# Attention and sticky mixture of experts on one core: the order of the tail's vector operations in the three early blocks, the place of two groups of small products, and the splitting of weight pieces

## The chip, the cores and the metric

The kernel runs on one core of a Trainium2 chip. The metric is the device time of one execution in microseconds. Three executions of the kernel before took 684.99, 685.71 and 685.96 us; the median, 685.71 us, is the time before. Apart from these one execution was profiled, and every view of the trace is of that one.

## The reference

Two stages follow one another. The first is attention for 8 batches and 8 heads of width 64. Each of 512 local tokens attends to 32 global tokens and to the local tokens at most 32 places away; each of the 32 global tokens attends to all 544. The outputs of all heads of a token stand side by side as a row of 512 numbers, 576 rows a batch, 4608 rows in all. The second stage sends each row through one of eight experts:

```python
logits = np.einsum('bsd,de->bse', x, w_gate)
local_gate = 1.0 / (1.0 + np.exp(-np.einsum('bsd,de->bse', x, w_local).squeeze(-1)))
out = np.zeros((B, S, D), dtype=np.float32)
for b in range(B):
    prev_e = -1
    for s in range(S):
        fresh_e = int(np.argmax(logits[b, s]))
        if s == 0 or local_gate[b, s] < 0.5:
            e = fresh_e
        else:
            e = prev_e if prev_e >= 0 else fresh_e
        prev_e = e
        ls = logits[b, s] - logits[b, s].max()
        p = np.exp(ls)
        p /= p.sum() + 1e-09
        h = np.maximum(x[b, s] @ w1[e], 0.0)
        out[b, s] = p[e] * (h @ w2[e])
```

An expert's w1 is 512 x 1024 and its w2 1024 x 512. Which expert a row takes depends on the rows before it, so the lists of rows per expert can only be complete when the last attention output is.

## The kernel before, in words

**Attention** fills roughly the first 229 us, unit by unit (a pair of heads of a batch). It is software-pipelined, and its last two units, the finishing of the last batch and the routing of its rows are not worked off there: they are collected in a generator, `Attn.tail`, that yields after each small chunk of work.

**Expert blocks.** A block takes 256 rows of one expert. Its first product, mm1 (L1274), runs over eight groups fc 0 to 7 of 128 columns of w1, of 12 matmuls each: four take the high half of the weights with the high half of x, four the low half of the weights, four the low half of x. All numbers are split in a high and a low part of reduced precision, so that three products together give the precision that is wanted. ACT makes the high part of the result (`hh`, L1276) and DVE the low part (`hl`, L1279). The second product, mm2 (L1287), runs over the same eight fc, three matmuls each, once for rows 0 to 127 (y0) and once for rows 128 to 255 (y1).

**Three early blocks** (i = 0, 1, 2) take rows of which the expert is known before the routing ends. Each has 24 places called hooks: hooks 0 to 7 behind the groups of mm1, 8 to 15 behind those of mm2 y0, 16 to 23 behind those of mm2 y1. I write (i, k) for hook k of block i. At a hook the kernel takes the next chunk of the tail, then `flush`es the subtraction that is pending, then splits new pieces as the table `SP[i][k]` says. The engines execute in the order in which this code issues, so the table and the yields of the tail fix each engine's order.

**Pieces.** A weight piece is a quarter of w1 or of w2 of an expert, 512 KB; a block needs eight. It is loaded to a `raw` buffer by a DMA on SP's queue, ACT casts its high half (L1173), and at the next hook's flush the low half is made by a subtraction (L1183), on DVE, or on POOL for two pieces split ahead of block 0. A flush frees the `raw` buffer and issues the next load. SP[2] names the pieces of the fourth block that are split within block 2.

**The tail**, in order: the last global unit's transposes (`g_t`) and its products with v (`g_av`, L342; its probabilities `ptg` come from ACT L332); the last local unit's transposes and products (`l_t`, L263; `l_av`, followed on DVE by L282, L284 and L287); the finishing of the outputs; the gate's keys (`keys`, L753, L824); ranking by a prefix scan (`pc`, L911) and products with ones (L875 to L884); probabilities (`probs`, L764 to L785); lists (`lists`, L924 and on); `kinds` (L1064 to L1087), eleven operations on DVE, the last of which writes `cnd`; and `rest`, the picking of the later lists: four groups of three DVE operations (L1000, L1002, L1004), each on 128 x 486 numbers, and then 34 small matmuls (L1010).

**The hint.** `cnd` holds for each of the eight blocks behind the early ones which case of a switch it takes. Every engine loads the first of them in a register at the same place of its program, ahead of mm2 y0 fc 4 of block 2:

```python
if mid and fc == 4:
    self.finish(True)
    while not self.known:
        self.take(next(self.tail))
    self.hint(i + 1)
```

Behind this, between the mm2 y1 groups of block 2, the rows of the fourth block are transposed four times (`xpose`, L1228, behind fc 2, 4, 5 and 6), each split by ACT (L1230) and DVE (L1231) into halves.

## Time and profile before

| what | value |
|---|---|
| median of three runs | 685.71 us (684.99 to 685.96) |
| the profiled execution's own time | 684.55 us |
| its span | 682.8 us |
| mean granted clock of TensorE | 0.995 |
| PE busy | 655.4 us, 96% of the span |
| DVE busy | 433.7 us, 64% |
| ACT busy | 342.1 us, 50% |
| POOL busy | 195.0 us, 29% |

A row of the timeline or of the list of groups gives start, duration, engine, line, operation, what it writes and reads, and how many instructions it stands for; a bracket at the end gives the idle time just ahead of it and what ended that. A row of the windows gives the stretch, its length, the busy time and instructions of PE, PE's weight loads, DVE, ACT and POOL, the granted clock, the DMA share and GB/s. A row of the waits gives the engine and line that waited, the one waited for, microseconds in total, how often, and the longest. Block 0 begins at about 229 us, block 1 at 267, block 2 at 290, and the fourth block at 323.

### The profile page before, as it was taken

To read this page: it belongs to the slowest core of one execution; us is meant where nothing else is said; L and a number is where in the kernel's file an instruction comes from. 1 tells how busy PE (TensorE), PEld (TensorE's weight loads), DVE (VectorE), ACT (ScalarE), POOL (GpSimd) and SP (SyncE) were. 2 spreads that over 40 slices of the span, in tenths; PEclk is the share of its full clock that TensorE was granted. 3 is DMA by queue.
4 is the path that set the end of the run, shared out by engine and by line. 5 is a ranking of instruction groups with operands and counts; after the bars stand their busy time and mean duration, and the time that the engine had idled before them with its cause. 6 is when DMAs were issued, how large, how long until landed. Compare 5 with 4: busy or idle time off the path is not lost.

```text
span 682.8 us, 18511 instructions
## 1 busy us (share of the span) xinstructions
PE 655.4 (96%) x7285; PEld 556.2 (81%) x7285; DVE 433.7 (64%) x1101; ACT 342.1 (50%) x614; POOL 195.0 (29%) x321
## 2 busy tenths in 40 slices
PE   8999999999999899998999899999999999999995
PEld 7778778777677787886987798989898989898994
DVE  7878778788887677988425553626374526355573
ACT  4555556555555574743427534435354425255563
POOL 7634334343324301031213304021123011133023
PEclk9999999999999999999999999999999999999998
DMA  8966967866757497766626674528283617265673
GB/s 321 405 217 249 336 216 305 316 247 237 303 188 291 135 353 255 259 206 200 254 89 223 212 246 151 183 82 265 86 297 120 235 63 236 93 218 182 222 276 102
DMA packets 42886, 151.47 MB, mean 222 GB/s; under 512 B 7837, under 2 KB 9117, under 8 KB 38560
## 3 DMA queue, kind: packets, MB, share of 16 engines
q1 hardware_dynamic: 35536, 126.92, 52.5%
q0 software_dynamic: 6832, 21.90, 9.5%
q8 instruction: 78, 1.28, 0.8%
q14 instruction: 152, 1.25, 0.6%
q10 hardware_dynamic: 288, 0.13, 0.1%
HBM read 130.55 MB, written 19.16 MB: 219 GB/s over the span
## 4 chain that ended last, share of the span: by engine, by line
PE 56%; DVE 6%; issue 1%; ACT 1%; POOL 0%; DVEq 0%; POOLq 0%; ACTq 0%
PE ps L1274 26%; PE ps L1287 23%; PE ps L1228 2%; PE ps L1293 2%; DVE wp L1183 1%; DVE wq L1183 1%; DVE xT L1002 0%; DVE xT L1000 0%; PE ps L1010 0%; DVE xl L1183 0%; ACT wp L1173 0%; DVE wp L1231 0%; POOL xa L1214 0%; DVE o L916 0%; DVE xl L1231 0%
## 5 line engine op out<-in xcount | busy, mean ns | idle before, releaser
L1306 POOL DMA_INDIRECT out_dram<-y,tk x39 | 40.8, 1045 | 309.5 <-ACT y L1305 221.7
L1287 PE MATMUL ps<-wp,wq 128*128 128x512 f32 x444 | 114.5, 403 | 1.0 <-ACT wq L1403 1.0
L1274 PE MATMUL ps<-wp,wp 128*128 128x256 f32 (+6 forms) x672 | 107.7, 320 | 0.0
L1274 PEld LDWEIGHTS ps<-wp,wp 128*128 128x128 f32 x672 | 103.5, 188 | 3.5
L1287 PEld LDWEIGHTS ps<-wp,wq 128*128 128x128 f32 x444 | 82.2, 190 | 18.1 <-ACT wq L1403 1.2
L1279 DVE SCALAR_TENSOR_TENSOR wq<-ps,wq 128x384 fp32r<-128x384 f32 (+4 forms) x112 | 43.5, 414 | 56.5 <-ACT wq L1276 48.0
L193 POOL TENSOR_SCALAR_AFFINE_SELECT qbd<-raw 64x512 f32<-64x512 f32 x62 | 44.3, 714 | 118.4 <-PE ps L246 92.2
L1276 ACT ACTIVATE wq<-ps 128x256 fp32r<-128x256 f32 (+6 forms) x80 | 36.9, 463 | 76.0 <-PE ps L1274 63.9
L246 PE MATMUL ps<-kx,qbd 128*64 128x128 f32 x1024 | 67.4, 275 | 1.3 <-issue 0.7
L1231 DVE TENSOR_TENSOR wp<-ps,wp 128x512 fp32r<-128x512 f32 x40 | 27.5, 691 | 58.3 <-ACT wp L1230 58.3
L257 ACT ACTIVATE pe<-pe 128x512 f32<-128x512 f32 x64 | 40.7, 636 | 43.8 <-DVE pe L253 43.8
L246 PEld LDWEIGHTS ps<-kx,qbd 128*64 128x64 f32 x1024 | 58.5, 138 | 2.1 <-POOL kx L193 1.1
L251 DVE TENSOR_REDUCE mx<-ps 128x4 f32<-128x512 f32 x64 | 43.8, 685 | 24.3 <-PE ps L246 24.1
L1183 DVE TENSOR_TENSOR wp<-raw,wp 128x1024 fp32r<-128x1024 f32 x47 | 57.0, 1217 | 2.9 <-ACT wp L1173 2.8
L1214 POOL DMA_INDIRECT xa<-xs,idx x42 | 50.2, 1194 | 18.8 <-issue 8.5
L1305 ACT ACTIVATE y<-ps,pp 128x512 f32<-128x512 f32 x35 | 24.2, 690 | 60.3 <-PE ps L1287 48.4
L1173 ACT CAST wp<-raw 128x1024 fp32r<-128x1024 f32 x49 | 50.9, 1047 | 1.3 <-ACT hh L1276 0.5
L1230 ACT CAST wp<-ps 128x512 fp32r<-128x512 f32 x40 | 23.5, 589 | 50.1 <-PE ps L1228 49.9
L253 DVE TENSOR_TENSOR pe<-ps,mx 128x512 f32<-128x512 f32 x64 | 44.0, 687 | 1.6
L279 PEld LDWEIGHTS ps<-v,pt 128*32 128x32 f32 x2048 | 33.1, 110 | 14.1 <-issue 7.9
L279 PE MATMUL ps<-v,pt 128*32 128x65 f32 x2048 | 41.7, 222 | 2.1 <-DVE xa L287 1.1
L193 POOL TENSOR_SCALAR_AFFINE_SELECT kx<-raw 128x384 f32<-128x384 f32 (+3 forms) x127 | 42.6, 368 | 3.1 <-DMA raw<-in_qk_dram 1.0
(296 smaller groups left out, 1188.2 us busy)
## 6 DMA issues: line engine op xcount, KB each, us to landing
raw<-in_w_dram SPq DMA_DIRECT2D x78, 512.0 KB, 4.4
v<-in_vw_dram SPq DMA_DIRECT2D x32, 1040.0 KB, 9.2
raw<-in_qk_dram SPq DMA_DIRECT2D x32, 528.0 KB, 7.8
xa<-in_w_dram SPq DMA_DIRECT2D x26, 512.0 KB, 4.2
xT<-in_w_dram SPq DMA_DIRECT2D x20, 512.0 KB, 5.1
xs<-xa SPq DMA_DIRECT2D x8, 1056.0 KB, 5.9
qgb<-in_qg_dram SPq DMA_DIRECT2D x8, 128.0 KB, 4.7
xa<-xs,idx POOLq DMA_INDIRECT x42
```

The costliest lines, as they stand in the source:

```text
L193: self.nc.gpsimd.affine_select(out=out, in_=in_, pattern=pat, compare_op=ALU.is_ge, fill=0.0, base=0, channel_multiplier=0)
L246: nc.tensor.matmul(sp[64 * t2:64 * t2 + 64, t], qbd[:, w], kf[:, f:f + P], start=False, stop=True, skip_group_check=True)
L251: nc.vector.tensor_reduce(out=mx, in_=st["sp"], axis=AX.X, op=ALU.max)
L253: nc.vector.tensor_tensor(out=st["pe"][:, 4 * hb:4 * hb + 4], in0=st["sp"], in1=mx.broadcast_to([P, 4, P]), op=ALU.subtract)
L279: nc.tensor.matmul(o[32 * w4:32 * w4 + 32, g, h], pt[:, 2 * g + w4 // 2, w4 % 2, h, :], v[:, w, h * (D + 1):(h + 1) * (D + 1)], start=True ...
L1173: nc.scalar.copy(out=hi, in_=raw)
L1183: (nc.gpsimd if pool else nc.vector).tensor_tensor(out=lo, in0=raw, in1=hi.bitcast(F32), op=ALU.subtract)
L1214: self.nc.gpsimd.indirect_dma_start(out=self.xr[j] if k == "early" else self.xr4[:, j], out_offset=None, in_=src, in_offset=bass.IndirectO ...
L1274: nc.tensor.matmul(ph, a[:, dc, fs], b_[:, dc, n0:n1], start=(n == 0), stop=(n == 11))
L1279: nc.vector.scalar_tensor_tensor(out=o[:, fc, c:c + b_ - a], in0=ph[:, a - n0:b_ - n0], scalar=0.0, in1=hh[:, fc, a:b_].bitcast(F32), op0= ...
L1287: nc.tensor.matmul(py, a[:, fc, js], b_[:, fs], start=(fc == 0 and k == 0), stop=(fc == 7 and k == 2))
L1306: sc = nc.gpsimd.indirect_dma_start(out=self.out, out_offset=bass.IndirectOffsetOnAxis(ap=tk[rows, js], axis=0), in_=y[rows], in_offset=No ...
```

## The change

Five edits touch only the order of the work; the operations are the same and equally many.

- In `tail`, `yield from lag(2)` stands for one yield ahead of `g_av`, and the yield behind `alloc_a` is gone. So the products with v move from hook (0,1) to hook (0,2), into the same chunk as `l_t`.
- In the ranking of the last batch, six yields are put between the scan and the ranking products. Three yields of this generator pass at one hook, so the products move two hooks, from (0,22) to (1,0), and what follows them in the tail (probabilities, lists, kinds) comes two hooks later too. Kinds move from hooks (2,5) to (2,8) to hooks (2,7) to (2,10).
- Three operations of `rest` come early: one behind each three operations of `kinds`. The other nine follow behind `kinds` as before, two a hook.
- `SP[0]`: the splits at hooks 1, 2, 3, 4 stand at 2, 3, 4, 5.
- `SP[2]`: hook 14 is dropped, so that six pieces of the fourth block are split within block 2, where it were seven.

```diff
--- before.py
+++ after.py
@@ -535,11 +535,10 @@
         b = B - 1
         fin = [x for x in fin if x[0] is not None]
         self.g_t(sg)
-        yield
+        yield from lag(2)
         self.g_av(sg)
         self.at2.close()
         moe.alloc_a()
-        yield
         self.l_t(sl, 0)
         self.l_t(sl, 1)
         yield
@@ -570,9 +569,12 @@
         self.f4(b, rt)
         yield from every(rt.lists(self.ps_o), 2)
         yield LISTS
-        yield from every(rt.kinds(), 3)
+        r = rt.rest(self.ps_o)
+        for _ in every(rt.kinds(), 3):
+            next(r)
+            yield
         yield KINDS
-        yield from every(rt.rest(self.ps_o), RE)
+        yield from every(r, RE)
@@ -871,6 +873,7 @@
             nc.vector.tensor_copy(self.sumA, pc[:, :, n - 1])
             yield
         else:
+            yield from lag(6)
             cp = po()
@@ -1530,9 +1533,9 @@
-SP = [_sp({1: 1, 2: 1, 3: 1, 4: 1, 6: 1, 7: 1, 10: 1, 13: 1, 15: 1, 19: 1}),
+SP = [_sp({2: 1, 3: 1, 4: 1, 5: 1, 6: 1, 7: 1, 10: 1, 13: 1, 15: 1, 19: 1}),
       _sp({0: 1, 1: 1, 2: 1, 3: 1, 5: 1, 7: 1, 8: 1, 11: 1, 13: 1, 15: 1, 17: 1, 19: 1}),
-      _sp({1: 1, 3: 1, 5: 1, 7: 1, 10: 1, 12: 1, 14: 1})]
+      _sp({1: 1, 3: 1, 5: 1, 7: 1, 10: 1, 12: 1})]
```

In the changed file the lines behind the first edits have numbers three higher or so: L1274 is L1277 there, L1183 is L1186, L1279 is L1282, L1287 is L1290.

**Three places in the engines' order.** The first is DVE in block 0, behind mm1 fc 1. L345 to L349 finish the products with v, L1279 is the low part of a group of mm1, L1183 the subtraction of a piece, and L282 to L287 finish the last local unit. Before:

```order
L345 TENSOR_SCALAR rsg_125<-ps_69 128x1
L347 RECIPROCAL rsg_125<-rsg_125 128x1
L349 TENSOR_SCALAR xg_111<-ps_69,rsg_125 128x64
L1279 SCALAR_TENSOR_TENSOR hl<-ps_63,hh 128x256
L1183 TENSOR_TENSOR wp_4271<-raw_79,wp_4271 128x1024
L1279 SCALAR_TENSOR_TENSOR hl<-ps_65,hh 128x256
L282 TENSOR_SCALAR rs_123<-ps_70 128x4
L284 RECIPROCAL rs_123<-rs_123 128x4
L287 TENSOR_TENSOR xa_109<-ps_70,rs_123 128x2x128
L1183 TENSOR_TENSOR wp_4272<-raw_80,wp_4272 128x1024
```

And with the change:

```order
L1282 SCALAR_TENSOR_TENSOR hl<-ps_63,hh 128x256
L345 TENSOR_SCALAR rsg_125<-ps_69 128x1
L347 RECIPROCAL rsg_125<-rsg_125 128x1
L349 TENSOR_SCALAR xg_111<-ps_69,rsg_125 128x64
L1282 SCALAR_TENSOR_TENSOR hl<-ps_65,hh 128x256
L282 TENSOR_SCALAR rs_123<-ps_70 128x4
L284 RECIPROCAL rs_123<-rs_123 128x4
L287 TENSOR_TENSOR xa_109<-ps_70,rs_123 128x2x128
L1186 TENSOR_TENSOR wp_4285<-raw_79,wp_4285 128x1024
L1282 SCALAR_TENSOR_TENSOR hl<-ps_66,hh 128x256
```

The three operations behind the products with v now stand behind the low part of fc 2, and the third piece (index 2) is subtracted where the fourth was, behind the finishing of the local unit.

The second is PE between the last groups of block 0 and the first of block 1, with the ranking products. Before:

```order
L1287 MATMUL ps_64<-wp_4377,hh 128x512 x2
L1287 MATMUL ps_64<-wp_4377,hl 128x512
L875 LDWEIGHTS on
L875 MATMUL ps_69<-sumA,on 128x8
L876 LDWEIGHTS on
L876 MATMUL ps_69<-pc,on 128x8
L881 LDWEIGHTS nlt
L881 MATMUL ps_70<-oh,nlt 128x104
```

And with the change:

```order
L1290 MATMUL ps_64<-wp_4374,hh 128x512 x2
L1290 MATMUL ps_64<-wp_4374,hl 128x512
L1277 MATMUL ps_65<-xh,wq_4375 128x256 x8
L1277 MATMUL ps_65<-xl,wq_4375 128x256 x4
L878 LDWEIGHTS on
L878 MATMUL ps_69<-sumA,on 128x8
L879 LDWEIGHTS on
L879 MATMUL ps_69<-pc,on 128x8
L884 LDWEIGHTS nlt
```

The products now stand behind mm2 fc 7 of block 0 and behind the whole of mm1 fc 0 of block 1.

The third is DVE in block 2, around the operations of `kinds`. The L1279 with ps_66 that stands in both pieces is the one of fc 7, the last of mm1. Before:

```order
L1183 TENSOR_TENSOR wp_4271<-raw_78,wp_4271 128x1024
L1279 SCALAR_TENSOR_TENSOR hl<-ps_66,hh 128x256
L1078 TENSOR_SCALAR kb<-kq 1x8
L1081 TENSOR_SCALAR kt<-kq 1x8
L1083 TENSOR_TENSOR kt<-kt,kb 1x8
L1085 SCALAR_TENSOR_TENSOR kt<-left,kt 1x8
L1087 TENSOR_TENSOR cnd<-kt,kb 1x8
L1183 TENSOR_TENSOR wp_4272<-raw_79,wp_4272 128x1024
L1000 TENSOR_TENSOR xT<-cid,phi 128x9x54
```

And with the change, from the same L1279 on, first up to the subtraction:

```order
L1282 SCALAR_TENSOR_TENSOR hl<-ps_66,hh 128x256
L1067 TENSOR_SCALAR eid<-ek 1x13
L1069 TENSOR_TENSOR eoh<-ge 128x104
L1071 TENSOR_SCALAR cnd<-lim 1x1
L1003 TENSOR_TENSOR xT<-cid,phi 128x9x54
L1074 TENSOR_SCALAR kq<-cn 1x8
L1076 TENSOR_SCALAR kq<-kq 1x8
L1078 TENSOR_SCALAR kq<-kq 1x8
L1005 TENSOR_TENSOR xT<-xT,t_266 128x9x54
L1186 TENSOR_TENSOR wp_4286<-raw_79,wp_4286 128x1024
L1081 TENSOR_SCALAR kb<-kq 1x8
```

and then to the end of `kinds`:

```order
L1084 TENSOR_SCALAR kt<-kq 1x8
L1086 TENSOR_TENSOR kt<-kt,kb 1x8
L1007 TENSOR_SCALAR xT<-xT,ipf 128x9x54
L1088 SCALAR_TENSOR_TENSOR kt<-left,kt 1x8
L1090 TENSOR_TENSOR cnd<-kt,kb 1x8
L1003 TENSOR_TENSOR xT<-cid,phi 128x9x54
L1005 TENSOR_TENSOR xT<-xT,t_266 128x9x54
```

All eleven operations of `kinds`, three of `rest` and a subtraction now stand between the low part of fc 7 and the `cnd` that the hint loads; before it were the last five of `kinds`.

## The prediction

> **What bounds the kernel now.** I first read the page's busy times: PE is the engine that sets the end.
>
> ```profile
> PE 655.4 (96%) x7285; PEld 556.2 (81%) x7285; DVE 433.7 (64%) x1101; ACT 342.1 (50%) x614; POOL 195.0 (29%) x321
> ```
>
> The change leaves the work of PE as it is, and so it can only move PE's idle time and what hangs on it. Next I cut the span into windows by block, and listed the waits of PE from 226 to 323 us, the stretch that the change touches.
>
> ```profile
> 290.00:323.00 33.00, 28.42 (x234) 25.03 (x233) 27.80 (x59) 14.18 (x22) 8.60 (x7) 1.00 0.66 205
> PE ps L1228 <- DVE wp L1231: 2.2, 1, 2.2
> PE ps L1274 <- DVE hl L1279: 1.7, 1, 1.7
> PE ps L342 <- ACT ptg L332: 1.7, 1, 1.7
> PE ps L876 <- DVE pc L911: 1.1, 1, 1.1
> ```
>
> Block 2 (290 to 323) has DVE busy for 27.80 of 33.00 us: there DVE is nearly as full as PE (28.42). Two of the four large waits are on DVE's backlog there. Four waits sum to 6.7 us, about 1% of the span; the edits are put at three of them (L342, L876, L1228). A wait that is removed pays only if nothing stands right behind it. So I walk each place in order of time, with the lateness of PE against before carried along.
>
> **The products with v, one chunk later.**
>
> ```profile
> 235.27 0.93 PE L342 MATMUL ps<-v,ptg 128*32 128x65 f32 x48 [1.66 <-ACT ptg L332]
> 237.08 0.74 PE L1274 MATMUL ps<-xh,wp 128*128 128x256 f32 x4 [0.20 <-POOL wp L1183]
> 234.65 2.37 POOL L1183 TENSOR_TENSOR wp<-raw,wp 128x1024 fp32r<-128x1024 f32 x1 [4.37 <-DVE gx L785]
> ```
>
> The wait of 1.66 us looks like the prize. But the group of mm1 that comes behind (fc 2) needs the low half of its piece, which POOL finishes at 234.65 + 2.37 = 237.02, and PE does start it at 237.08, after a last wait of 0.20. Before, the products filled part of the time until then. Moved behind fc 2 they leave that time idle, since fc 2's low weights come no earlier. So nothing is gained, and the products' own time (235.27 to the next group's start 0.87 later) is added behind: **+0.9**. Its bounds are 0 (if POOL were to start earlier; its 4.37 of idle end with an operation of DVE that doesn't move) and +0.9.
>
> **Pieces split one hook later in block 0.** The products with v and the finishing of the local unit stand ahead of the subtraction of the third piece in DVE's new order, and its place is where the fourth piece's is now.
>
> ```profile
> 241.11 1.22 PE L1274 MATMUL ps<-xh,wp 128*128 128x256 f32 x8
> 239.09 1.22 DVE L1183 TENSOR_TENSOR wp<-raw,wp 128x1024 fp32r<-128x1024 f32 x1
> 241.84 0.42 DVE L287 TENSOR_TENSOR xa<-ps,rs 128x256 f32<-128x256 f32 x1
> 242.19 1.22 DVE L1183 TENSOR_TENSOR wp<-raw,wp 128x1024 fp32r<-128x1024 f32 x1
> 267.10 11.53 PE ps L1274 x96
> ```
>
> PE begins fc 4, the first group of the third piece, at 241.11, or 241.98 with the 0.87 before. A matmul takes 11.53 / 96 = 0.12, so the four with the high half last until 242.5. The low half came at 239.09 + 1.22 = 240.3, well ahead. Now it starts behind L287, at 242.19 + 0.87, and ends 1.22 later, at 244.28. PE waits 244.28 - 242.46 = **+1.8**. The bounds are +0.9 (L282 to L287 don't depend on the later products, so the 0.87 may not be added in full) and +1.8; I take the upper one, because L279, which they read, is behind the products on PE. DVE and PE then run equally late, so the fourth piece adds no further wait. The flush also issues the next load on SP's queue, one hook, some 1.5 us, later:
>
> ```profile
> raw<-in_w_dram SPq DMA_DIRECT2D x78, 512.0 KB, 4.4
> ```
>
> A load lands in 4.4 us and is not needed before block 0's mm2, over 5 us later; I cost it at nothing, and at up to 1.5 if that cover is gone. Together PE is now 2.7 us late.
>
> **The ranking products, two hooks later.**
>
> ```profile
> 264.72 0.18 PE L875 MATMUL ps<-sumA,on 128*128 128x8 bf16 x1
> 265.58 0.38 DVE L911 TENSOR_TENSOR_SCAN pc<-segb,rv 128x104 bf16<-128x104 f32 x1
> 266.01 0.17 PE L876 MATMUL ps<-pc,on 128*128 128x8 bf16 x1 [1.10 <-DVE pc L911]
> ```
>
> The scan ends at 265.96, at worst 2.7 later: 268.7. The products now stand behind mm2 fc 7 (three matmuls at 0.23, from the nine in 2.11 shown below: 0.7) and a whole group of twelve (1.44): 264.72 + 2.7 + 0.7 + 1.44 = 269.6. The wait goes: **-1.1**, and nothing takes its place here. PE is 1.6 late.
>
> **What follows the ranking moves into DVE's full stretch.**
>
> ```profile
> 265.87 0.18 DVE L764 TENSOR_TENSOR lpr<-L,lm 128x40 f32<-128x40 f32 x1
> 268.99 0.43 DVE L1279 SCALAR_TENSOR_TENSOR hl<-ps,hh 128x256 fp32r<-128x256 f32 x1 [1.79 <-ACT hh L1276]
> 270.43 0.42 DVE L1279 SCALAR_TENSOR_TENSOR hl<-ps,hh 128x256 fp32r<-128x256 f32 x1 [0.61 <-ACT hh L1276]
> 296.21 1.08 DVE L1279 SCALAR_TENSOR_TENSOR hl<-ps,hh 128x256 fp32r<-128x256 f32 x3
> ```
>
> DVE's operations for the probabilities ran from 265.87 to 268.99 - 1.79 = 267.20, ahead of an idle time of 1.79. Two hooks later these 1.3 us stand behind the low part of mm1 fc 0, and only the 0.61 ahead of fc 1 is still free; behind 270.43 DVE goes without a break to the three low parts at 296.21 for which mm1 of block 2 waits 1.7. DVE gets there 1.6 (PE's lateness) + 1.3 later, less what the 0.61 absorbs: 2.3 to 2.9; I take 2.6, **+1.0** on PE beside the 1.6. The bounds are 0 (all absorbed) and +1.3.
>
> **`kinds`, three operations of `rest` and the hint.** From the order: behind the low part of fc 7 DVE now has all of `kinds`, three operations of `rest` and a subtraction before `cnd` is written.
>
> ```profile
> 303.10 0.15 DVE L1064 TENSOR_SCALAR eid<-ek 1x13 int32<-1x13 f32 x1
> 303.35 0.14 DVE L1068 TENSOR_SCALAR cnd<-lim 1x1 int32<-1x1 f32 x1
> 304.45 0.15 DVE L1071 TENSOR_SCALAR kq<-cn 1x8 int32<-1x8 int32 x1
> 305.02 1.21 DVE L1183 TENSOR_TENSOR wp<-raw,wp 128x1024 fp32r<-128x1024 f32 x1
> 306.15 0.41 DVE L1279 SCALAR_TENSOR_TENSOR hl<-ps,hh 128x256 fp32r<-128x256 f32 x1
> 306.49 0.15 DVE L1078 TENSOR_SCALAR kb<-kq 1x8 f32<-1x8 int32 x1
> 307.12 0.16 DVE L1087 TENSOR_TENSOR cnd<-kt,kb 1x8 int32<-1x8 f32 x1
> 308.35 0.66 DVE L1000 TENSOR_TENSOR xT<-cid,phi 128x486 bf16<-128x486 bf16 x1
> 309.04 0.67 DVE L1002 TENSOR_TENSOR xT<-xT,t 128x486 bf16<-128x486 bf16 x1
> 309.74 0.36 DVE L1004 TENSOR_SCALAR xT<-xT,ipf 128x486 bf16<-128x486 bf16 x1
> 308.52 0.72 PE L1287 MATMUL ps<-wq,hh 128*128 128x512 f32 x2 [0.68 <-ACT wp L1173]
> ```
>
> The wait of 0.68 at 308.52 is named after ACT, but ACT's cast is not what comes last: it is the place of the hint, `cnd` was written at 307.28, and PE goes on 1.24 later. So this wait hangs on `cnd`. Its new time: the low part of fc 7 begins at 306.15 + 2.6 = 308.75. Behind it come by these rows 0.34, 0.39, 0.57 and 0.79 for itself and the three parts of `kinds`, 0.66 + 0.67 + 0.36 of `rest` and 1.13 to 1.21 of the subtraction: 4.9 to 5.0. Neighbours on DVE overlap (1.21 us of a subtraction take 1.13 from start to start), so I take 4.5, with 4.2 and 5.0 as bounds. `cnd` is written at 313.25, PE goes on at 314.5 instead of 308.52: 6.0 late, of which **+3.4** is new here. PE would arrive at 307.84 + 2.6 = 310.4 and idle for 4.0 us instead of 0.68. Behind the same load stand ACT and POOL, whose program holds it too; ACT's casts and `hh` are finished ahead of it, so nothing else becomes late by more than PE.
>
> **The fourth block's transposes, and six pieces.**
>
> ```profile
> 316.88 1.22 DVE L1183 TENSOR_TENSOR xl<-raw,xh 128x1024 fp32r<-128x1024 f32 x1
> 318.01 1.28 DVE L1231 TENSOR_TENSOR wp<-ps,wp 128x512 fp32r<-128x512 f32 x2
> 318.75 0.66 PE L1228 MATMUL ps<-idf,xa 128*128 128x128 f32 x4 [2.23 <-DVE wp L1231]
> ```
>
> The third transpose waits for the first L1231, which stands behind DVE's backlog. With PE 6.0 late the transpose comes at 318.75 - 2.23 + 6.0 = 322.5. DVE has, behind `cnd`, nine operations of `rest` (three times 1.7) and a subtraction (1.1), with small ones some 7 us: free at 320.3, and the first L1231 done by 321. This wait goes: **-2.2**. That a seventh subtraction (1.22 at 316.88) is gone from this stretch helps nothing any more; with that piece the slack of 1.5 would still do. The seventh piece is now split in the fourth block, whose mm2 needs it tens of microseconds later, and each later block again splits eight, so I cost it at nothing (1.1 if DVE were late there).
>
> Sum: 0.9 + 1.8 - 1.1 + 1.0 + 3.4 - 2.2 = **+3.8** us.
>
> **The clock.** Idle time of 4.0 us has a price of its own here, seen later in the same trace:
>
> ```profile
> 374.00:378.00 4.00, 1.65 (x10) 0.93 (x10) 3.66 (x6) 2.99 (x7) 0.00 (x0) 1.00 0.91 294
> 378.00:382.00 4.00, 3.50 (x9) 2.76 (x10) 1.53 (x2) 0.00 (x0) 0.00 (x0) 0.60 0.83 302
> 378.50 3.90 PE ps L1287 x9
> 402.56 2.11 PE ps L1287 x9
> ```
>
> After a stretch in which PE was busy for 1.65 of 4.00 us (41%) the granted clock fell to 0.60 on the mean of the next 4 us, and nine matmuls took 3.90 us where the chain has 2.11 for the same nine elsewhere: a loss of 1.8. An idle time of 4.0 leaves some stretch of that length with PE idle for at least half of it wherever the stretches begin, so I expect one such drop behind the hint: **+1.8** (bounds 0 and 1.8). The Trainium skill, "TensorE: Matmul & The Clock Gate", section "What's actually happening", says that the clock halves after at least one idle window of about 3.4 us, and that these windows run freely. Read strictly, a window with a matmul in it would not count; the drop in this trace, after a stretch with 41% of work, speaks for a looser reading. By the strict one an idle time of 4.0 us holds a whole window in about one case of five only, and the sum would stay at +3.8; that is the first rival.
>
> **Forecast**: +3.8 + 1.8 = +5.6 on the profiled execution's 684.55 us (span 682.8), about 690.1; the profiled execution lay 1.2 below the median, so on 685.71 it is **691.2** (rounded down, as most of the bounds lie lower). The work behind block 2 keeps PE as full as before, so no later slack returns it.
>
> **Rivals.**
> - *No drop of the clock.* For it: the two recorded halves of one idle time may fall into two stretches that each have enough work. Against: the row above. 685.7 + 3.8 = 689.5.
> - *Two or three drops.* The waits in block 0 (POOL's piece, 2.5 us idle around 236, and 1.8 at 243) and at mm1 of block 2 (1.7 + 1.0 = 2.7) are idle times of over 40% of such a stretch too. Each costs 1.2 to 1.8 more: 692.5 to 694.
> - *DVE's idle time takes in what is moved.* If the third piece is subtracted in time and `cnd` comes no later, because DVE reaches `kinds` early (it had 0.63 to 1.79 of idle ahead of some low parts), only the products' 0.9 is left: 686.6, no change that can be told.
> - *The named waits simply go*, the other side: L342, L876 and L1228 lose 1.66 + 1.10 + 2.23 with no lateness put in their place, so that PE is ahead and the hint's load is met in time: 680.7. It decides if `cnd` is written before PE arrives, that is, if the eleven operations of `kinds` begin before fc 7's low part. Against: the order puts all eleven behind it, and 4.5 us on DVE stand against 2.8 us that PE needs for the twelve matmuls of mm2 fc 0 to 3.
> - *A load comes late.* The issue of the next weights moves a hook, 1.5 us, in block 0: +1 to +2 on the forecast, 692 to 693.
>
> **How the numbers follow.** Forecast 0.42, no drop 0.20, more drops 0.20, late load 0.04, no change 0.08, faster 0.06. A difference of less than 0.2% (1.4 us, that is 684.3 to 687.1) can't be told from no change. The likeliest case's own range is 690.0 to 692.3: the bounds of the hint's 4.2 to 5.0, of DVE's backlog and of the third piece. The range of eight in ten reaches down past the case with no drop and its bounds and up to the second drop: 687.8 to 693.9. Chances: faster 0.06, same 0.08, slower 0.86.
>
> **What would show it.** In the profile of the changed kernel: at fc 4 of block 0 PE waits some 1.8 us for DVE's subtraction, and the wait of L342 is gone while fc 2 still ends its wait on POOL; no wait at the ranking products; at mm1 of block 2 a wait on the low part of 2.5 or so; behind fc 3 of mm2 in block 2 about 4 us of idle PE, whatever releaser is named, with `cnd` written some 1.2 ahead of its end; then a stretch of half clock; and L1228 without a wait. I am wrong on the price if `cnd` comes before 311, and on the clock if the windows behind the hint show 1.00.

## The result

The changed kernel takes 690.03 us (median of ten executions, 687.47 to 695.13), the kernel before 685.45 us beside it (683.36 to 688.42). The ratio is 1.0071 with a 95% interval of 1.0052 to 1.0089: slower by 4.6 us, within 3.6 to 6.1. Put beside the kernel before a second time, it gave 1.0067 (1.0046 to 1.0088). The forecast was 691.2 us, 5.5 above.

The profiled execution took 688.34 us, its span 686.6. The waits of PE from 226 to 328 us in the changed kernel, to be laid beside the four of before:

```profile
PE ps L1290 <- DVE xT L1003: 3.3, 1, 3.3
PE ps L1277 <- DVE hl L1282: 2.4, 1, 2.4
PE ps L1277 <- POOL wp L1186: 2.1, 2, 1.7
PE ps L1277 <- DVE wp L1186: 1.7, 1, 1.7
PE ps L1277 <- ACT wp L1176: 1.0, 1, 1.0
```

Three of the waits of before are gone from the list (the products with v, the ranking products, the fourth block's transposes). In their place stand two at mm1 fc 2 of block 0, one for ACT's cast (1.0) and one for POOL (1.7 of the 2.1), so that PE still waits where it waited ahead of the products with v; one at mm1 fc 4 of block 0 (1.7); and one at the hint (3.3 where it was 0.7). The one at mm1 of block 2 grew from 1.7 to 2.4. The rows in PE's order of time:

```profile
233.70 0.74 PE L1277 MATMUL ps<-xh,wp 128*128 128x256 f32 x4 [1.00 <-ACT wp L1176]
236.13 1.23 PE L1277 MATMUL ps<-xh,wp 128*128 128x256 f32 x4 [1.69 <-POOL wp L1186]
238.14 1.39 PE L342 MATMUL ps<-v,ptg 128*32 128x65 f32 x48
244.89 0.74 PE L1277 MATMUL ps<-xh,wp 128*128 128x256 f32 x4 [1.66 <-DVE wp L1186]
271.69 0.18 PE L879 MATMUL ps<-pc,on 128*128 128x8 bf16 x1
301.54 1.22 PE L1277 MATMUL ps<-xh,wp 128*128 128x256 f32 x8 [2.45 <-DVE hl L1282]
316.03 0.72 PE L1290 MATMUL ps<-wq,hh 128*128 128x512 f32 x2 [3.34 <-DVE xT L1003]
323.88 0.60 PE L1231 MATMUL ps<-idf,xa 128*128 128x128 f32 x4
```

L342, L879 and L1231 have no bracket any more. On DVE, these are the low part of fc 7 and the last operation of `kinds`, which writes `cnd`:

```profile
310.43 0.42 DVE L1282 SCALAR_TENSOR_TENSOR hl<-ps,hh 128x256 fp32r<-128x256 f32 x1
314.64 0.15 DVE L1090 TENSOR_TENSOR cnd<-kt,kb 1x8 int32<-1x8 f32 x1
```

From the one's start to the other's end are 4.36 us (forecast 4.5, before 1.13), and PE goes on at 316.03, 1.24 after `cnd`, as before. The low part of fc 6, just ahead, waits for ACT in both kernels, here before and with the change:

```profile
304.11 0.42 DVE L1279 SCALAR_TENSOR_TENSOR hl<-ps,hh 128x256 fp32r<-128x256 f32 x1 [0.63 <-ACT hh L1276]
```

```profile
308.96 0.42 DVE L1282 SCALAR_TENSOR_TENSOR hl<-ps,hh 128x256 fp32r<-128x256 f32 x1 [1.60 <-ACT hh L1279]
```

**The clock.** In windows of 4 us the changed kernel shows half clock at two places of block 0, and none behind the hint:

```profile
233.00:237.00 4.00, 1.60 (x8) 1.40 (x9) 1.46 (x7) 1.97 (x5) 2.35 (x1) 0.85 0.01 2
237.00:241.00 4.00, 4.00 (x68) 3.68 (x68) 1.03 (x4) 1.18 (x3) 0.00 (x0) 0.72 0.98 305
245.00:249.00 4.00, 4.00 (x49) 3.70 (x50) 2.15 (x5) 1.32 (x2) 0.00 (x0) 0.63 0.55 200
314.00:318.00 4.00, 1.97 (x9) 1.65 (x10) 3.88 (x11) 1.05 (x1) 0.00 (x0) 1.00 0.71 232
```

In windows of 1 us every such stretch of every profile adds up to 3.4 us at half clock, or to twice that. The profile before has one ahead of the program's end (at 378), the changed kernel three (235, 246, and 382 in the half case).

**Where the time went.** The waits and the places between them can be laid side by side by a few rows that every profile has: the start of POOL's second subtraction (L1183), the keys' transposes (L824), the first group of block 1, the group of mm1 in block 2 that waits for DVE, the row at which PE goes on behind the hint, the fourth block's first group, and the first group of the block behind the half case. Differences of their starts, in us; a star is a stretch of half clock that falls into it:

| from, to | before | before again | after | after again |
|---|---|---|---|---|
| POOL's subtraction, keys (block 0) | 24.48 | 26.13* | 30.21** | 28.83* |
| keys, block 1 | 7.81 | 7.79 | 6.28 | 6.27 |
| block 1, the group that waits in block 2 | 29.74 | 29.73 | 31.32 | 31.31 |
| that group, PE behind the hint | 11.84 | 11.83 | 14.49 | 14.50 |
| hint, fourth block | 14.16 | 14.17 | 11.73 | 13.35* |
| fourth block, behind the half case | 64.25* | 64.27* | 63.45* | 63.72* |

Where no star differs, repeated profiles agree within 0.02 us in all but the last row. So the waits belong to the order of the work; the stretches of half clock come and go. Without them block 0 takes 27.4 (the run with `rest` behind `kinds`, below, which is the changed kernel in all that stands ahead), and the change comes to +2.9 - 1.5 + 1.6 + 2.65 - 2.4 - 0.8 = **+2.4 us**. Between the two first profiles this leaves 1.4 us: two stretches of half clock in block 0 add 2.8 (30.21 against 27.4), 0.9 is saved ahead of POOL's subtraction, in the attention, which no edit touches, and 0.5 behind the last matmul. Together that is 3.8, the difference of the spans (686.6 and 682.8). Between the medians, 4.6 apart, the other 2.2 can only be put down to the clock by its mean; "Adding up" below does that.

### The profile page after: what moved, and what is told of

Its sections match the earlier page's. It is cut to its first block, busy times and chain, and to the rows that moved or that the text cites. A ratio compares the mean times of both kernels' runs of the same rounds, so it can differ in the third digit from the quotient of the medians.

```text
span 686.6 us, 18494 instructions
## 1 busy us (share of the span) xinstructions
PE 658.7 (96%) x7285; PEld 559.6 (81%) x7285; DVE 432.6 (63%) x1100; ACT 340.8 (50%) x613; POOL 195.8 (29%) x321
## 4 chain that ended last, share of the span: by engine, by line
PE 56%; DVE 6%; issue 1%; DMA 1%; SPq 1%; ACT 1%; POOL 0%; POOLq 0%
PE ps L1290 25%; PE ps L1277 25%; PE ps L1231 3%; PE ps L1296 2%; DVE wp L1186 2%; DVE wq L1186 1%; DMA xs<-gx 1%; DVE hl L1282 1%; SPq L420 1%; PE ps L1415 0%; PE ps L1013 0%; POOL xa L1217 0%; DVE o L919 0%; DVE xl L1234 0%; ACT wp L1176 0%
## 5 line engine op out<-in xcount | busy, mean ns | idle before, releaser
L1290 PE MATMUL ps<-wp,wq 128*128 128x512 f32 x444 | 114.4, 403 | 1.0 <-ACT wq L1406 1.0
L1277 PE MATMUL ps<-wp,wp 128*128 128x256 f32 (+6 forms) x672 | 107.7, 320 | 0.0
L1277 PEld LDWEIGHTS ps<-wp,wp 128*128 128x128 f32 x672 | 103.5, 188 | 3.5
L1290 PEld LDWEIGHTS ps<-wp,wq 128*128 128x128 f32 x444 | 82.3, 191 | 18.2 <-ACT wq L1406 1.2
L1282 DVE SCALAR_TENSOR_TENSOR wq<-ps,wq 128x384 fp32r<-128x384 f32 (+4 forms) x112 | 43.3, 412 | 58.5 <-ACT wq L1279 54.3
L1279 ACT ACTIVATE wq<-ps 128x256 fp32r<-128x256 f32 (+6 forms) x80 | 37.0, 464 | 75.9 <-PE ps L1277 64.5
L1186 DVE TENSOR_TENSOR wp<-raw,wp 128x1024 fp32r<-128x1024 f32 x38 | 46.1, 1216 | 2.8 <-ACT wp L1176 2.8
L1176 ACT CAST wp<-raw 128x1024 fp32r<-128x1024 f32 x40 | 41.4, 1045 | 3.6 <-DVE xT L1003 3.6
```

The costliest lines, as they stand in the source:

```text
L1176: nc.scalar.copy(out=hi, in_=raw)
L1186: (nc.gpsimd if pool else nc.vector).tensor_tensor(out=lo, in0=raw, in1=hi.bitcast(F32), op=ALU.subtract)
L1277: nc.tensor.matmul(ph, a[:, dc, fs], b_[:, dc, n0:n1], start=(n == 0), stop=(n == 11))
L1282: nc.vector.scalar_tensor_tensor(out=o[:, fc, c:c + b_ - a], in0=ph[:, a - n0:b_ - n0], scalar=0.0, in1=hh[:, fc, a:b_].bitcast(F32), op0= ...
L1290: nc.tensor.matmul(py, a[:, fc, js], b_[:, fs], start=(fc == 0 and k == 0), stop=(fc == 7 and k == 2))
```

## The experiments

Each of the first four undoes one part of the changed kernel.

**Block 0 undone, both edits:**

```diff
-        yield from lag(2)
+        yield
         self.g_av(sg)
         self.at2.close()
         moe.alloc_a()
+        yield
-SP = [_sp({2: 1, 3: 1, 4: 1, 5: 1, 6: 1, 7: 1, ...
+SP = [_sp({1: 1, 2: 1, 3: 1, 4: 1, 6: 1, 7: 1, ...
```

> The changed kernel with both edits of block 0 undone (products with v one chunk earlier, splits at hooks 1, 2, 3, 4). Theory 1, lateness is carried on: the 3.3 us by which PE enters block 1 late in the changed kernel go (its first group at 265.5 to 266 instead of 270.2), and the hint and the transposes of the fourth block move with them: PE goes on behind the hint near 312 instead of 316.0, and the time is 3 to 4 us shorter than the changed kernel's, 686 to 687. Theory 2, DVE's backlog behind the ranking decides when cnd is written, whatever block 0 does: block 1 begins earlier but the wait at the hint grows by as much, and the time falls by less than 1 us, 689 to 690.

Measured: 685.34 us, ratio 1.0003 (0.9980 to 1.0026) to before. That is 4.5 below the changed kernel's 1.0067 to 1.0071, and theory 1. Block 1 begins at 263.47, even earlier than expected, since this execution's attention ended sooner (POOL's subtraction at 232.71, 233.73 in the changed kernel). The waits behind it are the same:

```profile
294.79 1.26 PE L1278 MATMUL ps<-xh,wp 128*128 128x256 f32 x8 [2.45 <-DVE hl L1283]
310.74 1.21 PE L1291 MATMUL ps<-wq,hh 128*128 128x512 f32 x2 [3.32 <-DVE xT L1004]
```

So the lateness of block 0 is carried on one to one, and the waits of DVE's backlog (2.45 and 3.3) are added to it. The 310.74 would be 309.3 without the half clock that this profile shows behind the first of the two waits; two stretches more, one right after the other, begin within the second wait, at 309.5:

```profile
295.00:299.00 4.00, 4.00 (x23) 4.00 (x23) 1.95 (x4) 1.32 (x2) 0.00 (x0) 0.61 0.09 35
311.00:315.00 4.00, 4.00 (x10) 3.13 (x11) 3.93 (x7) 0.66 (x1) 0.00 (x0) 0.50 0.57 201
```

**Only the products with v put back**, the first of the two diffs above without the table:

> The changed kernel with only the products with v put back one chunk earlier; the splits stay one hook later. Theory 1: the products again fill 0.9 us of the wait for POOL's piece; the wait at mm1 fc 4 for the subtraction stays at 1.7; block 1 begins 0.9 to 1.9 earlier (the latter if one stretch of half clock goes with it), and the time is as much shorter, 688 to 689. Theory 2 (DVE's backlog decides at the hint): within 0.5 of the changed kernel, 689.5 to 690.

Measured: 687.15 us, ratio 1.0035 (1.0012 to 1.0059), about 2.3 below the changed kernel, theory 1 and a little more. (The profiled execution, 682.74, is the shortest of the ten.) Block 0 takes 26.41 here with no half clock, 27.38 without the undoing: the products' new place costs 0.97, and the splits one hook later 1.93.

```profile
232.87 0.93 PE L342 MATMUL ps<-v,ptg 128*32 128x65 f32 x48 [0.87 <-ACT ptg L332]
234.67 0.74 PE L1278 MATMUL ps<-xh,wp 128*128 128x256 f32 x4 [0.20 <-POOL wp L1187]
241.10 0.74 PE L1278 MATMUL ps<-xh,wp 128*128 128x256 f32 x4 [1.67 <-DVE wp L1187]
```

The products stand in the wait for POOL again, and the wait at fc 4 stays.

**The ranking products two hooks earlier again** (`yield from lag(6)` taken out):

> The changed kernel without the six yields ahead of the ranking products: they and all that follows stand two hooks earlier again, with three operations of rest still among kinds. Theory 1: the wait of 1.1 at the ranking products is back, the wait at mm1 of block 2 falls from 2.4 to about 1.7, and the wait at the hint from 3.3 to about 1, since only the last two or three operations of kinds and one of rest stand behind the low part of fc 7: 2 us shorter in all, 688. Rival: the operations of rest, not the two hooks, make the hint late; then the wait there stays over 2 us and the time is that of the changed kernel or, with the 1.1, longer, 690 to 691.

Measured: 683.70 us, ratio 0.9983 (0.9966 to 1.0000). The mechanism is theory 1's, the size isn't: 5.8 us below the changed kernel where 2 were expected. The trace shows the waits as expected:

```profile
PE ps L1276 <- DVE hl L1281: 1.7, 1, 1.7
PE ps L1289 <- DVE wp L1185: 1.4, 1, 1.4
PE ps L878 <- DVE pc L913: 1.1, 1, 1.1
```

By the rows of the table the hint is 2.0 us earlier, the ranking and block 2 are as before, and the transposes keep their gain: 0.5 above before in all, 1.9 below the changed kernel. The mean granted clock may make up the rest: 0.9949 over ten executions, 0.9916 for the kernel before beside it. That isn't shown, since among these ten the time hardly goes with the clock (683.45 us at 0.999, 681.98 at 0.995).

**`rest` behind `kinds` again:**

```diff
-        r = rt.rest(self.ps_o)
-        for _ in every(rt.kinds(), 3):
-            next(r)
-            yield
+        yield from every(rt.kinds(), 3)
         yield KINDS
-        yield from every(r, RE)
+        yield from every(rt.rest(self.ps_o), RE)
```

> The changed kernel with all of rest behind kinds, as before. Theory 1: cnd comes earlier by the three operations of rest ahead of it (0.57 + 0.57 + 0.27, 1.4 to 1.7 us), the wait at the hint falls from 3.3 to 1.7, and the transposes of the fourth block give back at most 0.3: 1.2 to 1.6 us shorter, 688.5. Rival: what is taken from the hint comes back in full as a wait of the transposes for DVE (L1234): no difference, 690.

Measured: 686.28 us, ratio 1.0021 (0.9996 to 1.0046), about 3 below the changed kernel, where 1.2 to 1.6 were expected. Theory 1 in kind: the wait at the hint is 2.1 instead of 3.3, and the transposes wait as little as in the changed kernel, so nothing comes back there.

```profile
313.10 0.96 PE L1287 MATMUL ps<-wq,hh 128*128 128x512 f32 x2 [2.13 <-DVE xT L1000]
```

**Six early pieces alone, on the kernel before:**

```diff
-      _sp({1: 1, 3: 1, 5: 1, 7: 1, 10: 1, 12: 1, 14: 1})]
+      _sp({1: 1, 3: 1, 5: 1, 7: 1, 10: 1, 12: 1})]
```

> The kernel before with one edit alone: six early pieces in block 2. Theory 1: the subtraction that ends at 318.1 no longer stands ahead of the first L1231, the wait of 2.2 at the third transpose falls to 1.1, and the time is 1.1 us shorter than before, ratio 0.9984. Rival: the operations of rest keep DVE as long, so that the wait and the time stay, ratio 1.000.

Measured: 680.07 us, ratio 0.9924 (0.9899 to 0.9949): faster than before by 5 us, where 1.1 were expected. The mechanism is there at its size, and a second one that I hadn't seen stands in the half case. From the fourth block's start to the block behind it, profiles with one stretch of half clock take 63.08 to 63.72 us with six pieces (five of them) and 64.19 to 64.27 with seven (three). First the transposes' wait in this kernel:

```profile
317.71 0.66 PE L1228 MATMUL ps<-idf,xa 128*128 128x128 f32 x4 [1.09 <-DVE wp L1231]
```

Then a wait in the half case, in the kernel before and in the changed one, both by time:

```profile
370.18 0.44 PE L1401 MATMUL ps<-idf,gsb 128*128 128x128 f32 x2 [0.85 <-ACT gsb L1415]
```

```profile
374.66 0.44 PE L1404 MATMUL ps<-idf,gsb 128*128 128x128 f32 x2 [0.24 <-ACT gsb L1418]
```

With six pieces that wait is gone or 0.24, with seven it is 0.85: one piece fewer is split before the half case, and its place in ACT's and DVE's order moves. So the six pieces take 1.1 + some 0.8 = 1.9 off the trace. Where the other 3 us come from is not shown. The mean clock is higher, 0.9955 beside 0.9912. But the profiled execution, which has no half clock ahead of the program's end (0.998), is the longest of the six (682.48): its half case takes 63.46 all the same, since PE waits 2.33 us at the next block's entry.

**Six pieces and three operations of `rest` among `kinds`, on the kernel before** (the two diffs above, the second the other way round):

> The kernel before with two edits: six early pieces, and three operations of rest among kinds; block 0 and the ranking as before. Theory 1: without the two hooks only some 0.7 us are added ahead of cnd (wait at the hint 1.4, as in the run without the six yields), and the wait of 2.2 at the transposes is gone: 1.5 us shorter than before, ratio 0.998. Rival: the operations of rest make the hint late by their full 1.7, which takes back what the transposes give: ratio 1.000.

Measured: 679.67 us, ratio 0.9925 (0.9900 to 0.9950), no different from six pieces alone. The waits are theory 1's:

```profile
307.38 0.72 PE L1290 MATMUL ps<-wq,hh 128*128 128x512 f32 x2 [1.40 <-DVE wp L1186]
```

and no wait at the transposes. Both are faster than the kernel before and the changed one. Here the profile says more of the rest. It and the first of before have one stretch of half clock each, at the half case, and lie near the medians (679.69 and 684.55). Their spans differ by 4.9 us: 0.7 more at the hint, 2.4 less at the transposes, 1.2 less in the half case, and 1.9 less ahead of POOL's subtraction, in the attention, which none of the edits touches. In before that subtraction begins at 234.65; in this profile, and in the run with seven pieces further below:

```profile
232.79 2.39 POOL L1186 TENSOR_TENSOR wp<-raw,wp 128x1024 fp32r<-128x1024 f32 x1 [3.58 <-DVE gx L788]
```

```profile
236.94 2.36 POOL L1186 TENSOR_TENSOR wp<-raw,wp 128x1024 fp32r<-128x1024 f32 x1 [4.37 <-DVE gx L787]
```

Over the 14 profiles its start lies between 232.2 and 236.9, by 0.3 and 0.6 between two profiles of one kernel. So a profile's span moves by more than most of these effects without the clock and without an edit.

**The clock, waits filled with work of no use.** `fill` issues matmuls whose results nothing reads:

```diff
+    def fill(self, n, bank, a, b):
+        for _ in range(n):
+            self.nc.tensor.matmul(bank[:, 0:256], a, b, start=True, stop=True)
...
+            if (i, fc) in FILL:
+                self.fill(FILL[i, fc], self.ph.t[self.ph.k % len(self.ph.t)], ...)
             self.mm1(i, fc, *x, 0, 256)
...
+                self.fill(FILL[i], self.ph.t[0], ...)
                 self.hint(i + 1)
```

> The changed kernel with matmuls of no use (results overwritten or never read) put where PE waits: 14 of 128 x 256 ahead of mm1 fc 2 and 12 ahead of fc 4 of block 0, 22 ahead of the hint's load. They take 1.7, 1.4 and 2.6 us, less than the waits there. The waits stay as long in all, but PE is no longer idle. Theory, that short idle times let the clock fall and that this is part of the change's price: no stretch of half clock in block 0 and behind the hint, and 1.5 to 3 us shorter than the changed kernel (ratio to before 1.003 to 1.005 in place of 1.007). Rival, that the stretches have another cause or that the work of no use delays as much: ratio 1.007 or more.

Measured: 692.23 us, ratio 1.0111 (1.0085 to 1.0137): above the changed kernel's 1.0067 to 1.0071, the intervals just touching, and against the theory by the total. The profile shows why the total can't decide it. Block 0 takes 27.41 with no half clock, and there is none behind the hint, as the theory has it:

```profile
234.00:238.00 4.00, 3.43 (x70) 3.04 (x69) 1.03 (x4) 0.94 (x3) 0.68 (x1) 1.00 0.57 135
314.00:318.00 4.00, 4.00 (x19) 3.32 (x18) 3.90 (x8) 0.83 (x2) 0.78 (x1) 1.00 0.45 157
```

But at the entry of the fourth block, a jump to a case of the switch, PE stands still for 3.8 us, and nothing that the profile shows is what it waits for:

```profile
328.94 5.35 PE L1278 MATMUL ps<-wp,wp 128*128 128x456 f32 x17 [3.81 <-issue]
```

and half clock comes four times elsewhere (298, 329, and twice from 383). The run is inconclusive on the price of the clock.

**Six pieces, and the three waits at the end of the half case filled:**

```diff
+        self.xpose(i + 1, 0)
+        self.fill(6, spare, *some)
+        self.xpose(i + 1, 1)
+        self.fill(8, spare, *some)
         turn(3)
+        self.fill(7, spare, *some)
```

> The kernel before with six early pieces, and with 6, 8 and 7 matmuls of no use at the three waits of PE at the end of the fourth block's half case (0.81, 1.08 and 0.97 us), behind which the profile before has a stretch of half clock. Theory: that stretch goes, 1.7 us less than with the six pieces alone, ratio 0.996. Rival: the stretch comes at the next idle time or is as frequent as before, ratio 0.998.

Measured: 680.47 us, ratio 0.9936 (0.9910 to 0.9961), no better than the six pieces alone. Half clock at the half case is gone from the profile and the mean clock is up to 0.9977, but what it saves turns into a wait of PE at the next block's entry, as in the run with six pieces alone (2.33):

```profile
384.38 3.94 PE L1274 MATMUL ps<-wp,hh 128*128 128x352 f32 x23 [1.72 <-ACT wp L1230]
```

The kernel before has 0.19 there. So a stretch of half clock in the half case is covered by something else: with one the part takes 63.08 us (six pieces and `rest` among `kinds`), with none 63.46 (six pieces alone). The 1.8 us from which I took my price were not lost there in full.

**Seven pieces in the changed kernel** (the diff of the six pieces undone):

> The changed kernel with seven early pieces again. Theory 1, that the dropped piece is worth what it takes off a wait: the transposes have 1.0 us of slack in the changed kernel, so a subtraction of 1.2 more costs 0 to 0.5 us, ratio to the changed kernel 1.000 to 1.001 (to before 1.007). Rival, from the run with six pieces alone, which was 4.9 us faster than before while its trace shows 1.1: the piece costs 4 to 5 us in any order, ratio to before 1.013.

Measured: 692.24 us, ratio to before 1.0094 (1.0067 to 1.0122), 0.27% above the changed kernel beside it; the intervals overlap. The rival's 1.013 lies outside the interval, theory 1's 1.007 at its edge. The trace has no wait at the transposes, as theory 1 said, and 0.86 for ACT in the half case, as before; the mean clock is 0.9877, the changed kernel's 0.9899.

**The wait of the transposes filled, in the kernel before:** 16 matmuls of no use ahead of the third transpose.

> The kernel before with 16 matmuls of no use (1.9 us) ahead of the third transpose of the fourth block, where PE waits 2.2 us for DVE. The wait stays as long in all, but PE is not idle. Theory, that this wait made the clock fall in most executions of the kernel before though not in the profiled one, and that this is the larger part of what six pieces gain: mean clock 0.0025 higher and 1.5 to 3 us shorter than before, ratio 0.996 to 0.998. Rival, that the gain of the six pieces has another cause: ratio 1.000.

Measured: 684.76 us, ratio 0.9995 (0.9981 to 1.0010). The rival: the wait itself shrinks to 0.36 behind the work of no use, and the time and the mean clock (0.9947 beside 0.9941) stay.

```profile
318.91 0.66 PE L1228 MATMUL ps<-idf,xa 128*128 128x128 f32 x4 [0.36 <-DVE wp L1231]
```

So the clock that six pieces gained was not lost at this wait. Where it was lost stays open.

**Both kernels once more:**

> The kernel before once more, for a second profile beside a timing. Theory of the clock: this profile shows two or three stretches of half clock ahead of the end, one of them likely behind the wait at 318.7, where the first profile has one in all. Rival: one stretch again, at the half case, and then the clock doesn't explain the six pieces.

> The changed kernel once more, on the chip of the other three. Theory: three or four stretches of half clock, in places that differ from the first profile's, with the same waits to 0.3 us (1.7 at fc 4 of block 0, 2.4 at mm1 of block 2, 3.3 at the hint, none at the transposes); ratio 1.005 to 1.009. Rival: the stretches stand at the same places, so that they belong to the order of the work and not to chance.

Measured: 686.38 (ratio 1.0015, 0.9999 to 1.0032) and 690.03 us (1.0067). The second profile of before has two stretches of half clock, one in block 0 (237) and one in the half case (381), and none behind the transposes, where I had put one. That of the changed kernel has three: one in block 0 instead of two, one behind the hint instead of none, one in the half case. The waits are the same to 0.1. So the stretches don't stand at fixed places of the program:

```profile
312.00:316.00 4.00, 0.79 (x4) 0.67 (x4) 3.90 (x10) 0.95 (x1) 0.00 (x0) 1.00 0.92 285
316.00:320.00 4.00, 4.00 (x12) 3.15 (x11) 3.90 (x8) 0.27 (x2) 0.00 (x0) 0.57 0.52 188
```

Here the same wait as at 316.03 in the first profile is followed by half clock; there it was not.

What tells the two apart is where the wait falls on a fixed grid. Within each profile the starts of all stretches lie whole multiples of 3.413 us apart (235.83, 246.07 and 382.61 in the changed kernel's first profile: 3 and 40 of them). So the span can be cut into windows of 3.41 us by that grid. The wait at the hint in the first profile, the same wait in the second, and the window behind the latter:

```profile
310.92:314.34 3.42, 1.77 (x8) 1.13 (x6) 3.32 (x12) 1.33 (x2) 1.37 (x2) 1.00 0.88 302
314.34:317.75 3.41, 1.72 (x8) 1.44 (x9) 3.34 (x8) 1.05 (x1) 0.00 (x0) 1.00 0.73 238
```

```profile
312.88:316.29 3.41, 1.08 (x5) 0.92 (x6) 3.31 (x10) 1.05 (x1) 0.00 (x0) 1.00 0.94 284
316.29:319.70 3.41, 3.41 (x10) 2.64 (x9) 3.34 (x7) 0.00 (x0) 0.00 (x0) 0.50 0.52 186
```

In the first the grid cuts the wait in two, and each window keeps 1.7 us of work. In the second most of the wait falls into one window, with 1.08 of work, and the next window runs at half clock. In the 14 profiles, from 20 us to about the last matmul, half clock follows each of the 18 full-clock windows in which PE was busy for 1.51 us or less, and none in which it was busy for more than 1.83. Between the two, 7 of 22 are followed by it, and nothing shown here tells these apart.

**Adding up.** A stretch costs 1.4 to 1.65 us in the rows of the table (26.13 against 24.48; 28.83 and 30.21 against 27.4), and 1.63 behind the hint; one stretch of 3.4 us at half clock lowers the mean clock of the span by 0.0025. So each kernel can be worked out as the trace's difference without stretches plus 1.5 us for each 0.0025 of mean clock below before, and laid beside what was measured:

| kernel | trace without half clock | mean clock, before's beside it | worked out | measured |
|---|---|---|---|---|
| changed, again | +2.4 | 0.9899, 0.9941 | +4.9 | +4.6 |
| block 0 undone | -0.5 | 0.9921, 0.9916 | -0.8 | +0.2 |
| products with v back | +1.4 | 0.9913, 0.9916 | +1.6 | +2.4 |
| ranking undone | +0.5 | 0.9949, 0.9916 | -1.5 | -1.2 |
| `rest` behind | +1.2 | 0.9923, 0.9916 | +0.8 | +1.4 |
| six alone | -1.9 | 0.9955, 0.9912 | -4.5 | -5.2 |
| six, `rest` among | -2.5 | 0.9942, 0.9912 | -4.3 | -5.1 |
| changed, seven | +3.2 | 0.9877, 0.9941 | +7.0 | +6.4 |
| before, filled | 0 | 0.9947, 0.9941 | -0.4 | -0.3 |

They agree within 1.0 us, in both directions. The run with six pieces and the half case filled, which isn't in the table, doesn't: the same working gives -5.8, and -4.4 was measured. The interval of each measured one is 1.0 to 1.9 us to a side, so this supports the account and doesn't prove it: no run took the half clock away from the changed kernel with nothing else moved. The price can also be read among executions of the same kernel. A line through the times and clocks of all 178, each kernel about its own mean, falls by 1.1 us for 0.0025 of clock, not by 1.5; among the 18 of the three kernels with six pieces and block 0 as before no such fall shows. So the clock is no sure account of what six pieces gain, and the attention, which also moves by some us, is a rival that no run here separates from it.

## Why the prediction was right, and where it wasn't

- **The products with v: right.** +0.9 forecast; the run with the products alone put back has 0.97, and fc 2 still ends its wait on POOL.
- **Pieces one hook later: right.** +1.8 forecast; 1.93, with a wait of 1.66 at fc 4. The DMA that moves with the flush cost nothing that the trace shows.
- **The ranking products: right.** -1.1 forecast, the wait is gone and nothing stands behind the products.
- **DVE's full stretch: right.** +1.0 forecast beside the -1.1, together -0.1; the two rows of the table give -1.5 + 1.6 = +0.1. The wait at mm1 of block 2 is 2.45.
- **The hint: mechanism right, the term mis-sized.** +3.4 forecast, 2.65 measured. The 4.36 us on DVE were right (4.5). The step that failed is "the low part of fc 7 begins at 306.15 + 2.6": three operations of `kinds` (304.45 to 305.02, 0.57 us) stood ahead of that low part before. In the new order they stand behind it, where I counted them, but the 306.15 still held them too: 0.57 counted twice. The low parts of fc 6, which wait for ACT in both kernels, are 4.85 apart, as much as PE is late there (301.54 against 296.68). The low parts of fc 7 are 4.28 apart (310.43 against 306.15). So PE reached the hint 2.26 us behind the start of that low part instead of 1.69 and idled 3.34, not 4.0.
- **The transposes: right.** -2.2 forecast, -2.4 measured.
- **Six pieces: mis-sized.** "I cost it at nothing": 0.8 in the half case was missed, where a wait for ACT falls from 0.85 to 0.24. Against the kernel before the piece also takes 1.1 off the transposes. In the changed kernel that is part of the -2.4, and the run with seven pieces in the changed kernel shows that they don't wait there with the seventh piece either.
- **The clock: the price near, place and certainty wrong.** I argued that a wait of 4.0 us would be followed by half clock "wherever the stretches begin", and named windows of 1.00 behind the hint as the sign against it; the changed kernel's first profile has them. Five profiles have a wait of 3.3 at the hint. Half clock follows it in two (the changed kernel's second profile, and the run with block 0 undone), and not in three (its first profile, the run with the products put back, the one with seven pieces). What failed here is the 4.0 once more. By the grid above, 4.0 us of idle would leave one of the two windows that it can touch with 1.4 us of work at most, under the 1.51 (an estimate from those counts). The 3.34 that came can leave up to 1.74 in each, where both happen. Block 0, which I had as a rival ("two or three drops"), shows it once or twice in most profiles that keep both of its edits, and once in the second profile of before. A stretch costs about 1.5, not 1.8: the 1.8 came from a stretch in the half case that was covered at the next block's entry. By mean clock the changed kernel has 1.7 stretches more than before, 1.9 to 2.5 us by the two prices above, where I had one, 1.8.

The stalls were forecast at +3.8 and came to +2.4; the clock at +1.8 and came to some +2 to +2.5 by the mean clock. The sum of 5.6 against 4.6 to 5.0 is right partly because these two errors have opposite signs. The rival "no drop" (689.5) lies nearest in time. Its mechanism, one idle time that falls into two stretches with enough work in each, is what the changed kernel's first profile shows at the hint. But its sum has no half clock at all, while block 0 has two stretches there, so that its nearness is luck as well.

On the clock the Trainium skill, "TensorE: Matmul & The Clock Gate", section "What's actually happening", says that half rate follows at least one idle window of about 3.4 us and that the windows run freely. Free-running fits: the stretches lie on a grid of 3.41 us in every profile, and the same wait is followed by one or not, as it falls on the grid. A window without any work isn't needed. In the second profile of before, half clock follows a window of the grid in which PE was busy for 1.83 us; in the first, a window of the same part of block 0 with 1.75 has full clock behind it:

```profile
234.18:237.59 3.41, 1.83 (x53) 1.53 (x54) 2.02 (x10) 2.91 (x6) 2.38 (x1) 1.00 0.00 0
```

```profile
232.03:235.44 3.41, 1.75 (x26) 1.55 (x28) 2.86 (x14) 2.43 (x5) 0.79 (x1) 1.00 0.32 126
```

This pair lies where both happen, and what tells it apart no row here shows.

## What to carry to other kernels

Of a wait that a list names, ask what stands next on the same engine and when that becomes ready: three waits of 5.0 us in all were removed here and 7.6 us came elsewhere (1.0 on ACT and 1.5 more on POOL at fc 2, 1.7 at fc 4, 0.8 at mm1 of block 2, 2.7 at the hint), because the pieces, the low part and `cnd` that PE needed next were set by ACT's, POOL's and DVE's order and not by the work that was moved. Moving work out of an engine's idle time into its full stretch added it here to that engine's later deadlines, mm1 of block 2 and the hint; at the hint a register load, which the list of waits named after ACT, was the deadline. And time small edits one by one: one of the five by itself made the kernel before 0.75% faster, and together with the other four it could not be seen.

## What I had not expected of the hardware

- Half clock comes in pieces of 3.4 us on a grid of that length, behind waits of 1.7 us as well as of 3.3, but not behind each: the work left in one window of the grid decides (in these profiles always at 1.51 us or less of 3.41, never above 1.83). Executions of one kernel spread by 1.7 to 7.7 us. Two profiles of the kernel before agree to 0.02 us in most stretches of the table, and their spans differ by 1.8 (682.8 and 684.6).
- Time saved ahead of the block behind the half case can be lost at its entry. PE waits there 0 to 0.6 us in eleven profiles, and 1.72, 2.05 (block 0 undone) and 2.33 in three. In these three it starts 0.14 after ACT's cast of the last transposed rows (L1230), so that ACT is what it waits for; why ACT comes so late there wasn't settled. The 3.8 us at the fourth block's entry in the filled run have no releaser at all.
